# TensorE pieces planned in longer runs of one tile size, the mask in 64-column tiles, and a second layer that trails by 5 steps instead of 6

## The chip, the cores and the metric

One core of a Trainium2 chip. The metric is device time in microseconds (us) of one execution.

## The reference

Two identical layers over 2048 tokens of width 512, each a segmented attention with 32 heads of 128 and a dense relu block. The attention goes over 64 segments of 32 tokens one after the other: 8 memory rows, which are the output of the segment before, stand ahead of the 32 tokens, so each segment waits for the one before it.

```python
for s in range(n_seg):                        # 64 segments
    h = concatenate([mem, xs])                # 8 + 32 rows
    q, k, v = h @ Wq, h @ Wk, h @ Wv          # 512 -> 32 heads x 128
    p = softmax(where(mask, q @ k.T * scale, -1e9))
    o = (p @ v) @ Wo                          # 32 x 128 -> 512
    mem = o[:8]; outs.append(o[8:])
# layer: x = x + attention(layernorm(x)); x = x + relu(layernorm(x) @ w1) @ w2      (twice)
```

## The kernel before

All operations are put into a plan in Python. A greedy list scheduler then fixes the order of each engine's instructions. One **step** handles segment k of layer 0 and segment k - DELTA of layer 1 together, so 64 + DELTA steps. Query/key products are on the critical recurrence; x-values (for the next step), memory values, x output and the dense layers fill TensorE in between.

```python
DELTA = 6
LAT = (0.26, 0.16, 0.16, 0.20, 1.70)      # signal latency charged behind PE, ACT, DVE, POOL, SP
LOOK = 0.05
...
# Plan.order(): rank = longest planned path to the end
            o.rank = o.cost + LAT[o.eng] + max((s.rank for s in o.succs), default=0.0)
...
            o = max((c for c in cand[e] if c.start <= lo + LOOK), key=lambda c: (c.rank, -c.seq))
            end = o.start + o.cost
            seen = end + LAT[e]
            for s in o.succs:
                s.ready = max(s.ready, seen)
...
# PSUM: eight banks; x-values, x output, dense layers and normalization share the two of "fill"
    b_qk, b_misc, b_st, b_fill = banks("qk", 2), banks("misc", 3), banks("st", 1), banks("fill", 2)
...
# x-values: each of the four contraction slices is a piece of its own (two 64-column tiles)
        for p in range(4):
            vx = b_fill.buf()
            for c4 in range(NC4):
                def mm(vx=vx, p=p, c4=c4): ...        # 2 matmuls, 512 columns
                plan.op(PE, 0.216, mm, r=[...], w=[vx, ("vst", p)] if c4 == 0 else [vx])
...
# x output: sixteen pieces that add up in one bank (four 32-column tiles each)
        wx = b_fill.buf()
        for t in range(H // 2):
            def mm(t=t): ...                          # 4 matmuls, 512 columns
            plan.op(PE, 0.216, mm, r=[("OT", t // 4), ("OT", 4 + t // 4), ("W", "o", 3)], w=[wx])
...
# mask: one whole-array matmul (identity x mask) ahead of scores in 64-column tiles
            nc.tensor.matmul(sp[:, a_lo * 4 * L:a_hi * 4 * L], lhsT=ident[:], rhs=maskb[...], start=True, stop=False)
```

## Time and profile before

| | before |
|---|---|
| time, median of 3 runs | 2491.64 us (2477.98 to 2494.26) |
| profiled execution | 2478.0 us, granted TensorE clock 0.979 |
| TensorE / VectorE / ScalarE / GpSimd busy | 93% / 49% / 30% / 14% |

A busy TensorE is not a TensorE at its peak, because the ends of matmuls are modelled. The starts are measured, and the prediction works with them: it splits the span into start, matmul stream, tile changes and waits.

### The profile page before, as it was taken

The page shows a single profiled execution, that of the slowest core. Times are in us where ns is not written, and L with a number is a line of the kernel's source. Part 1 is how long each engine was busy: PE and PEld are TensorE (multiplying, and loading weights), DVE is VectorE, ACT ScalarE, POOL GpSimd, SP SyncE. Part 2 cuts the span into 40 slices and gives each one's busy share as a digit, 9 for nine tenths or more (in the row PEclk, how much of TensorE's full clock was granted, in tenths as well). Part 3 has the DMA queues.
Part 4 walks back from the last instruction along what each step waited for, and adds up shares of the span by engine and source line. Part 5 has one row for each costly group of instructions (what it writes and reads, how often), then busy time and mean ns, then how long its engine had stood idle before and what let it go on. Part 6 is the DMA issues. An engine that isn't in the chain of part 4 may idle for free. (4 is left out here: it accounts for less than half of the span.)

```text
span 2478.0 us, 91607 instructions
## 1 busy us (share of the span) xinstructions
PE 2300.9 (93%) x40876; PEld 1338.7 (54%) x40876; DVE 1202.9 (49%) x2947; ACT 748.5 (30%) x1818; POOL 343.9 (14%) x910
## 2 busy tenths in 40 slices
PE   0899999999999999999999999999999999999998
PEld 0455555655555554555556554655556555555554
DVE  0334455545445545554545555554555455454443
ACT  0223332332333332333333332333323332323222
POOL 2101111111111111111111111111111111111110
PEclk9899999998999999999999999999999999999999
DMA  9000111101011101110111011101111011001000
GB/s 321 16 13 13 23 24 24 24 17 28 16 24 25 23 18 23 24 28 19 22 24 28 18 23 23 24 17 28 24 24 24 17 28 24 20 18 24 15 13 17
DMA packets 39259, 71.63 MB, mean 29 GB/s; under 512 B 13168, under 2 KB 20336, under 8 KB 38864
## 3 DMA queue, kind: packets, MB, share of 16 engines
q1 hardware_dynamic: 33296, 52.34, 9.6%
q8 instruction: 320, 5.24, 0.9%
q10 hardware_dynamic: 3824, 6.78, 0.8%
q0 software_dynamic: 1744, 6.65, 0.7%
q14 instruction: 75, 0.61, 0.1%
HBM read 21.70 MB, written 2.10 MB: 10 GB/s over the span
## 5 line engine op out<-in xcount | busy, mean ns | idle before, releaser
L535 PEld LDWEIGHTS <-Wk_sb 128*128 128x128 bf16 x8960 | 350.5, 99 | 100.8 <-issue 97.7
L535 PEld LDWEIGHTS <-Wq_sb 128*128 128x128 bf16 x8960 | 352.1, 99 | 90.5 <-issue 86.6
L697 PE MATMUL fill_184<-Wo_sb,OT 128*32 128x512 bf16 x2560 | 252.5, 389 | 2.6 <-DVE xg_74 L707 1.7
L659 PE MATMUL st_182<-Wo_sb,OT 128*32 128x512 bf16 x2208 | 225.0, 406 | 3.1 <-ACT OT L442 2.2
L442 ACT CAST QT<-qk_177 128x320 bf16<-128x320 f32 (+1 forms) x279 | 112.5, 403 | 380.1 <-PE qk_177 L535 375.4
L442 ACT CAST QT<-qk_178 128x320 bf16<-128x320 f32 (+1 forms) x281 | 113.5, 404 | 354.3 <-PE qk_178 L535 353.9
L444 DVE CAST KT<-qk_177 128x320 bf16<-128x320 f32 (+1 forms) x218 | 100.3, 460 | 240.9 <-PE qk_177 L535 226.9
L444 DVE CAST KT<-qk_178 128x320 bf16<-128x320 f32 (+1 forms) x202 | 92.7, 459 | 190.3 <-PE qk_178 L535 174.2
L697 PEld LDWEIGHTS <-OT 128*32 128x32 bf16 x4480 | 112.1, 94 | 134.7 <-issue 84.9
L605 POOL TENSOR_TENSOR P_145<-es_162,sm_166 128x160 bf16<-128x160 f32 (+1 forms) x140 | 58.1, 435 | 861.3 <-ACT QT L442 397.8
L697 PE MATMUL fill_183<-Wo_sb,OT 128*32 128x512 bf16 x1920 | 170.2, 385 | 0.0
L469 PE MATMUL fill_183<-Wv_sb,XS_139 128*64 128x512 bf16 x664 | 143.5, 428 | 1.9 <-ACT hT_176 L360 1.9
L535 PE MATMUL qk_177<-HT_136,Wk_sb 128*128 128x80 bf16 (+1 forms) x2256 | 124.7, 199 | 5.0 <-POOL HT_136 L460 4.9
L535 PE MATMUL qk_178<-HT_136,Wk_sb 128*128 128x80 bf16 (+1 forms) x2224 | 122.3, 199 | 4.1 <-POOL HT_136 L460 3.9
L469 PE MATMUL fill_183<-Wv_sb,XS_138 128*64 128x512 bf16 x632 | 125.3, 399 | 0.7
L535 PE MATMUL qk_178<-HT_136,Wq_sb 128*128 128x80 bf16 (+1 forms) x2256 | 125.1, 200 | 0.3 <-DVE KT L444 0.3
L535 PE MATMUL qk_177<-HT_137,Wk_sb 128*128 128x80 bf16 (+1 forms) x2240 | 123.0, 199 | 0.0
L535 PE MATMUL qk_177<-HT_136,Wq_sb 128*128 128x80 bf16 (+1 forms) x2224 | 122.8, 199 | 0.1
L535 PE MATMUL qk_178<-HT_137,Wk_sb 128*128 128x80 bf16 (+1 forms) x2240 | 122.9, 199 | 0.0
L535 PE MATMUL qk_177<-HT_137,Wq_sb 128*128 128x80 bf16 (+1 forms) x2240 | 122.9, 199 | 0.0
L535 PE MATMUL qk_178<-HT_137,Wq_sb 128*128 128x80 bf16 (+1 forms) x2240 | 122.8, 199 | 0.0
L469 PEld LDWEIGHTS <-XS_139 128*64 128x64 bf16 x1120 | 62.9, 112 | 105.4 <-issue 94.5
(205 smaller groups left out, 3829.2 us busy)
## 6 DMA issues: line engine op xcount, KB each, us to landing
Vs_142<-vst SPq DMA_DIRECT2D x128, 128.0 KB
Vs_143<-vst SPq DMA_DIRECT2D x128, 128.0 KB
Vs_142<-vms SPq DMA_DIRECT2D x256, 16.0 KB
Vs_143<-vms SPq DMA_DIRECT2D x256, 16.0 KB
Wk_sb<-in_A_Wk_dram ACTq DMA_DIRECT2D x2, 1024.0 KB
Wv_sb<-in_A_Wv_dram POOLq DMA_DIRECT2D x2, 1024.0 KB, 18.6
Wq_sb<-in_A_Wq_dram SPq DMA_DIRECT2D x2, 1024.0 KB
Wo_sb<-in_A_Wo_dram SPq DMA_DIRECT2D x2, 1024.0 KB
```

The costliest lines, as they stand in the source:

```text
L442: nc.scalar.copy(out=out_, in_=in_)
L444: nc.vector.tensor_copy(out=out_, in_=in_)
L469: nc.tensor.matmul(vx[64 * b:64 * b + 64, :], lhsT=XS[:, c4, :], rhs=Wv_sb[:, c4, n * 512:(n + 1) * 512], start=(c4 == 0), stop=(c4 == NC4 ...
L535: nc.tensor.matmul(qp[:, hi * 2 * L:hi * 2 * L + n], lhsT=W_sb[:, c4, h * Dh:(h + 1) * Dh], rhs=HT[:, c4, c0:c1], start=(c4 == 0), stop=(c ...
L605: nc.gpsimd.tensor_tensor(out=P[:, a_lo:a_hi, :, b, 0:L], in0=es[:, a_lo:a_hi, b, :, :], in1=s.unsqueeze(3).to_broadcast([128, na, 2, L]), ...
L659: nc.tensor.matmul(wo[32 * q:32 * q + 32, :], lhsT=OT[:, h, SEG:SEG + 32], rhs=Wo_sb[:, h, :], start=(t == 0), stop=(t == H // 4 - 1), til ...
L697: nc.tensor.matmul(wx[32 * q:32 * q + 32, :], lhsT=OT[:, h, XO[a]:XO[a] + SEG], rhs=Wo_sb[:, h, :], start=(t == 0), stop=(t == H // 2 - 1) ...
```

## The change

The intent is fewer changes of the TensorE tile (whole array, 64 columns, 32 columns, 64 rows). It has four parts: (1) pieces that add up in one bank are planned as one; (2) the planner charges 0.11 us for a change of tile, and a piece on the present tile gets 2 us of rank as a bonus; (3) the mask comes as two 64-column matmuls; (4) layer 1 trails by 5 steps.

```diff
-DELTA = 6
+DELTA = 5
+WHOLE, COL64, COL32, ROW64 = range(4)
+TURN = 0.11
+STAY = 2.0
...
-            o = max((c for c in cand[e] if c.start <= lo + LOOK), key=lambda c: (c.rank, -c.seq))
+            o = max((c for c in cand[e] if c.start <= lo + LOOK),
+                    key=lambda c: (c.rank + (STAY if e == PE and c.tile == tile else 0.0), -c.seq))
...
             end = o.start + o.cost
+            if e == PE and o.tile != tile:
+                end, tile = end + TURN, o.tile
...  x-values (memory values, queries/keys, memory output, dense layers likewise)
-            for c4 in range(NC4):
-                def mm(vx=vx, p=p, c4=c4):
+            def mm(vx=vx, p=p):
+                for c4 in range(NC4):
...
-                plan.op(PE, 0.216, mm, r=[...], w=[vx, ("vst", p)] if c4 == 0 else [vx])
+            plan.op(PE, 0.216 * NC4, mm, r=[...], w=[vx, ("vst", p)], tile=COL64)
...  x output: 4 pieces in place of 16
-        for t in range(H // 2):
+        for tq in range(4):
...
-            plan.op(PE, 0.216, mm, r=[("OT", t // 4), ("OT", 4 + t // 4), ("W", "o", 3)], w=[wx])
+            plan.op(PE, 0.864, mm, r=[("OT", tq), ("OT", 4 + tq), ("W", "o", 3)], w=[wx], tile=COL32)
...  mask
-            nc.tensor.matmul(sp[:, ...], lhsT=ident[:], rhs=..., start=True, stop=False)
+            for g2 in range(2):
+                nc.tensor.matmul(sp[64 * g2:64 * g2 + 64, ...], lhsT=ident[:, 64 * g2:64 * g2 + 64],
+                                 rhs=..., start=True, stop=False, tile_position=(0, 64 * g2))
```

More of the change, by code (lines that the diff above doesn't have):

```diff
@@ L73 @@
 class Op:
-    __slots__ = ("eng", "cost", "fn", "preds", "succs", "bufs", "new", "rank", "ready", "start", "wait", "seq")
+    __slots__ = ("eng", "cost", "fn", "preds", "succs", "bufs", "new", "rank", "ready", "start", "wait", "seq", "tile")
 class Plan:
@@ L83, in available, with op @@
         self.given[key] = t
-    def op(self, eng, cost, fn, r=(), w=()):
+    def op(self, eng, cost, fn, r=(), w=(), tile=WHOLE):
         o = Op()
-        o.eng, o.cost, o.fn, o.succs, o.seq = eng, cost, fn, [], len(self.ops)
+        o.eng, o.cost, o.fn, o.succs, o.seq, o.tile = eng, cost, fn, [], len(self.ops), tile
         o.ready, preds, o.bufs, o.new = 0.0, {}, [], []
@@ L124, in order @@
                 cand[o.eng].append(o)
-        done = []
+        done, tile = [], WHOLE
         while len(done) < len(self.ops):
@@ L346, in dense_layer, with mm @@
             hp = b_fill.buf()
-            for fi, fc in enumerate(fcs):
-                fs = 128 if fc < NFC - 1 else F_LAST
-                def mm(hp=hp, fi=fi, fc=fc, fs=fs):
+            def mm(hp=hp, fcs=fcs):
+                for fi, fc in enumerate(fcs):
+                    fs = 128 if fc < NFC - 1 else F_LAST
                     for c4 in range(NC4):
@@ L354, in mm @@
                                          rhs=xnT[:, c4, :], start=(c4 == 0), stop=(c4 == NC4 - 1))
-                plan.op(PE, 0.23, mm, r=[xnT, "w1"], w=[hp, hT] if fb == 0 and fi == 0 else [hp])
+            plan.op(PE, 0.23 * len(fcs), mm, r=[xnT, "w1", *([(hT, "own")] if fb else [])],
+                    w=[hp] if fb else [hp, hT, (hT, "own")])
             nfull = sum(1 for fc in fcs if fc < NFC - 1)
@@ L372, in dense_layer, with mm @@
             fcs = list(range(4 * fb, min(NFC, 4 * fb + 4)))
-            for two in range(0, len(fcs), 2):
-                def mm(part=fcs[two:two + 2]):
-                    for fc in part:
-                        fs = 128 if fc < NFC - 1 else F_LAST
-                        nc.tensor.matmul(yp[:, :], lhsT=hT[0:fs, fc, :], rhs=w2_sb[0:fs, fc, :],
-                                         start=(fc == 0), stop=(fc == NFC - 1))
-                plan.op(PE, 0.216 * len(fcs[two:two + 2]), mm, r=[hT, (hT, fb), "w2"], w=[yp])
+            def mm(fcs=fcs):
+                for fc in fcs:
+                    fs = 128 if fc < NFC - 1 else F_LAST
+                    nc.tensor.matmul(yp[:, :], lhsT=hT[0:fs, fc, :], rhs=w2_sb[0:fs, fc, :],
+                                     start=(fc == 0), stop=(fc == NFC - 1))
+            plan.op(PE, 0.216 * len(fcs), mm, r=[hT, (hT, fb), "w2"], w=[yp])
         def add():
@@ L471, in mm @@
                                          start=(c4 == 0), stop=(c4 == NC4 - 1), tile_position=(0, 64 * b))
-                plan.op(PE, 0.216, mm, r=[("XS", i, 0), ("XS", i, 1), ("W", "v", p)],
-                        w=[vx, ("vst", p)] if c4 == 0 else [vx])
+            plan.op(PE, 0.216 * NC4, mm, r=[("XS", i, 0), ("XS", i, 1), ("W", "v", p)], w=[vx, ("vst", p)], tile=COL64)
             eng = ACT if p != 3 else DVE
@@ L498, in mem_values, with mm @@
             vm = b_st.buf()
-            for c4 in range(NC4):
-                def mm(vm=vm, pp=pp, c4=c4):
+            def mm(vm=vm, pp=pp):
+                for c4 in range(NC4):
                     for q in range(4):
@@ L505, in mm @@
                                          start=(c4 == 0), stop=(c4 == NC4 - 1), tile_position=(0, 32 * q))
-                plan.op(PE, 0.216, mm, r=[("HTm", i), ("HTx", i, 1), *[("W", "v", pc) for pc in range(4)]], w=[vm])
+            plan.op(PE, 0.216 * NC4, mm, r=[("HTm", i), ("HTx", i, 1), *[("W", "v", pc) for pc in range(4)]], w=[vm],
+                    tile=COL32)
             eng = ACT if pp == 0 else DVE
@@ L529, in queries_keys, with mm @@
             qp = b_qk.buf()
-            for h2 in range(2):
-                def mm(qp=qp, h2=h2, W_sb=W_sb):
-                    for hi in (2 * h2, 2 * h2 + 1):
-                        h = 4 * hg + hi
-                        for c4 in range(NC4):
-                            nc.tensor.matmul(qp[:, hi * 2 * L:hi * 2 * L + n], lhsT=W_sb[:, c4, h * Dh:(h + 1) * Dh],
-                                             rhs=HT[:, c4, c0:c1], start=(c4 == 0), stop=(c4 == NC4 - 1))
-                plan.op(PE, 8 * max(0.030, 0.0029 + n / 2400), mm,
-                        r=[("HTm", i), *[("HTx", i, a) for a in range(a_lo, a_hi)], ("W", nm, hg // 2)], w=[qp])
+            def mm(qp=qp, W_sb=W_sb):
+                for hi in range(4):
+                    h = 4 * hg + hi
+                    for c4 in range(NC4):
+                        nc.tensor.matmul(qp[:, hi * 2 * L:hi * 2 * L + n], lhsT=W_sb[:, c4, h * Dh:(h + 1) * Dh],
+                                         rhs=HT[:, c4, c0:c1], start=(c4 == 0), stop=(c4 == NC4 - 1))
+            plan.op(PE, 16 * max(0.030, 0.0029 + n / 2400), mm,
+                    r=[("HTm", i), *[("HTx", i, a) for a in range(a_lo, a_hi)], ("W", nm, hg // 2)], w=[qp])
             eng = DVE if nm == "k" and hg % 4 != 1 else ACT
@@ L558, in mm @@
         def mm():
-            nc.tensor.matmul(sp[:, a_lo * 4 * L:a_hi * 4 * L], lhsT=ident[:],
-                             rhs=maskb[:, a_lo:a_hi, :].unsqueeze(2).to_broadcast([128, na, 4, L]),
-                             start=True, stop=False)
+            for g2 in range(2):
+                nc.tensor.matmul(sp[64 * g2:64 * g2 + 64, a_lo * 4 * L:a_hi * 4 * L],
+                                 lhsT=ident[:, 64 * g2:64 * g2 + 64],
+                                 rhs=maskb[:, a_lo:a_hi, :].unsqueeze(2).to_broadcast([128, na, 4, L]),
+                                 start=True, stop=False, tile_position=(0, 64 * g2))
             v = spv()
@@ L595, in scores @@
         qk = [(c + "T", hg) for c in "qk" for hg in (2 * p, 2 * p + 1)]
-        plan.op(PE, 0.07 * na + 8 * na * 0.0215, mm, r=qk, w=[sp])
+        plan.op(PE, 0.07 * na + 8 * na * 0.0215, mm, r=qk, w=[sp], tile=COL64)
         plan.op(DVE, t_dve(n), top, r=[sp], w=[mx])
@@ L639, in attend @@
                 r=[("PT", p), *[("Vx", a, b) for a in range(a_lo, a_hi) for b in range(2)],
-                   *[("Vm", a, 2 * (p // 2) + b) for a in range(a_lo, a_hi) for b in range(2)]], w=pv)
+                   *[("Vm", a, 2 * (p // 2) + b) for a in range(a_lo, a_hi) for b in range(2)]], w=pv, tile=ROW64)
         for b in range(2):
@@ L654, in next_memory, with mm @@
         wo, mt = b_st.buf(), b_misc.buf()
-        for t in range(H // 4):
-            def mm(t=t):
-                for q in range(4):
-                    h = 4 * t + q
-                    nc.tensor.matmul(wo[32 * q:32 * q + 32, :], lhsT=OT[:, h, SEG:SEG + 32], rhs=Wo_sb[:, h, :],
-                                     start=(t == 0), stop=(t == H // 4 - 1), tile_position=(0, 32 * q))
-            plan.op(PE, 0.216, mm, r=[("OT", t), ("W", "o", t // 2)], w=[wo])
+        for p in range(4):
+            def mm(p=p):
+                for t in (2 * p, 2 * p + 1):
+                    for q in range(4):
+                        h = 4 * t + q
+                        nc.tensor.matmul(wo[32 * q:32 * q + 32, :], lhsT=OT[:, h, SEG:SEG + 32], rhs=Wo_sb[:, h, :],
+                                         start=(t == 0), stop=(t == H // 4 - 1), tile_position=(0, 32 * q))
+            plan.op(PE, 0.432, mm, r=[("OT", 2 * p), ("OT", 2 * p + 1), ("W", "o", p)], w=[wo], tile=COL32)
         for half, eng in ((0, ACT), (1, DVE)):
@@ L692, in project_x, with mm @@
         wx = b_fill.buf()
-        for t in range(H // 2):
-            def mm(t=t):
-                for q in range(4):
-                    h, a = 16 * (q // 2) + t, q % 2
-                    nc.tensor.matmul(wx[32 * q:32 * q + 32, :], lhsT=OT[:, h, XO[a]:XO[a] + SEG], rhs=Wo_sb[:, h, :],
-                                     start=(t == 0), stop=(t == H // 2 - 1), tile_position=(0, 32 * q))
-            plan.op(PE, 0.216, mm, r=[("OT", t // 4), ("OT", 4 + t // 4), ("W", "o", 3)], w=[wx])
+        for tq in range(4):
+            def mm(tq=tq):
+                for t in range(4 * tq, 4 * tq + 4):
+                    for q in range(4):
+                        h, a = 16 * (q // 2) + t, q % 2
+                        nc.tensor.matmul(wx[32 * q:32 * q + 32, :], lhsT=OT[:, h, XO[a]:XO[a] + SEG],
+                                         rhs=Wo_sb[:, h, :], start=(t == 0), stop=(t == H // 2 - 1),
+                                         tile_position=(0, 32 * q))
+            plan.op(PE, 0.864, mm, r=[("OT", tq), ("OT", 4 + tq), ("W", "o", 3)], w=[wx], tile=COL32)
         for a in act:
```

## The prediction

> **What bounds the kernel now.** I read the first section of the page (busy time by engine) first, then the waits of TensorE, then TensorE's timeline over two steps, and last the distances between the starts of all 40,876 matmuls.
>
> The page's first section:
>
> ```profile
> PE 2300.9 (93%) x40876; PEld 1338.7 (54%) x40876; DVE 1202.9 (49%) x2947; ACT 748.5 (30%) x1818; POOL 343.9 (14%) x910
> ```
>
> TensorE is taken all the time and no other engine passes half. The waits of TensorE, longest first:
>
> ```profile
> PE fill_183 L326 <- DVE bf_76 L321: 60.1, 1, 60.1
> PE misc_181 L614 <- POOL P_148 L605: 17.4, 6, 2.9
> PE fill_184 L326 <- DVE bf_76 L321: 14.9, 10, 3.9
> ```
>
> The first is the start of the program (the loads), once. The second is the tail of some steps: the transposes of the last quarter of the heads wait for its softmax, and there is nothing left to fill. Everything below is smaller. So the bound is what TensorE does, and the question is how much of "busy" is work. That is read from the starts in the timeline. A stretch in which the tile changes at every group, then one in which it doesn't (columns: start, length, line, tiles, shape, count):
>
> ```profile
> 1206.91 0.45 PE L535 MATMUL qk_178<-HT_137,Wk_sb 128*128 128x80 bf16 x8
> 1207.30 0.40 PE L503 MATMUL st_182<-Wv_sb,HT_137 128*32 128x512 bf16 x4
> 1207.63 0.41 PE L469 MATMUL fill_183<-Wv_sb,XS_139 128*64 128x512 bf16 x2
> 1207.96 0.40 PE L503 MATMUL st_182<-Wv_sb,HT_137 128*32 128x512 bf16 x4
> 1208.29 0.41 PE L469 MATMUL fill_183<-Wv_sb,XS_139 128*64 128x512 bf16 x2
> ...
> 1210.94 0.30 PE L559 MATMUL misc_181<-maskb,ident 128*128 128x320 bf16 x1
> 1211.17 0.38 PE L569 MATMUL misc_181<-KT,QT 128*40 128x40 bf16 x16
> ...
> 1223.45 0.39 PE L697 MATMUL fill_183<-Wo_sb,OT 128*32 128x512 bf16 x4
> 1223.66 0.39 PE L659 MATMUL st_182<-Wo_sb,OT 128*32 128x512 bf16 x4
> 1223.88 0.39 PE L697 MATMUL fill_183<-Wo_sb,OT 128*32 128x512 bf16 x4
> 1224.10 0.39 PE L659 MATMUL st_182<-Wo_sb,OT 128*32 128x512 bf16 x4
> ```
>
> Four matmuls of 512 columns in 32-column tiles take 0.22 us from start to start when the next group has the same tile (1223.45 to 1223.66 to 1223.88), and 0.33 us when the next has another (1207.30 to 1207.63 to 1207.96). Eight query/key matmuls take 8 x 36 = 288 ns among their own kind, and 0.39 us ahead of another tile. The mask matmul (320 columns, 136 ns at the same rate) is followed after 0.23 us by scores in 64-column tiles. Each change costs about 0.10 us, and the modelled busy time hides it.
>
> Done over the whole span, by the distance of starts of consecutive matmuls less the distance that the same matmul has among its own tile (36 ns query/key, 56 ns at 128 columns, 216 ns at 512, 136 ns mask, 22 ns score or value matmul; over 160 ns of excess counted as a wait), the 2478.0 us fall into: 64.3 before the first query, 1779 of matmul stream, 468 of tile changes (4,658 of them, 100 ns each) and 167 of waits. The median excess of the pairs of tiles lies between 84 and 120 ns, whichever way they change. Of the steady steps, eight in a row (1437.44 to 1720.15 us) give 35.3 us a step: 26.2 stream, 6.6 changes (67 of them), 2.3 waits. Of the waits in all full steps the largest known ender is that of the last softmax quarter (38 us over 58 steps).
>
> **What the Trainium skill says.** "TensorEngine Tiling (Array Packing)", section Key Properties: changing the tiling mode, and not just the tile, drains TensorE. The trace agrees: 100 ns a change, none between two different 32-column groups. "TensorE: Matmul & The Clock Gate", section Back-to-back issue gap, gives N/2.4 + 2.5 ns for an isolated stream, 36 ns at 80 columns and 216 at 512: the trace has 36 and 216. The same page, "Part 3: Packing small matmuls — row/col tiling", has tiles of one mode starting some 4 ns apart; here 3 ns, so two mask matmuls of 64 columns of the array should cost about what one of 128 does. "Perfetto Trace Analysis", section Tensor Engine Instruction (MATMUL, LD_WEIGHTS), says that matmul ends in a profile are estimated; hence I use starts.
>
> **The change part by part.**
>
> *Merging of planned pieces.* The matmuls stay the same in number and size; what the planner may not split any more grows. Pieces per full step before: 32 query/key, 16 x-values, 8 memory values, 4 masks, 4 scores, 4 attention, 8 memory output, 16 x output, 4 transposes of P, 1 selection, 5.5 + 3 dense, 1 transpose of x: 106, with 67 changes, 0.63 a piece. After: 16 + 4 + 2 + 4 (mask and scores are one tile now) + 4 + 4 + 4 + 4 + 1 + 1.5 + 1.5 + 1 = 47 pieces. At the same 0.63 that is 30 changes.
>
> *The bonus for staying (2 us of rank).* It lets pieces of near rank follow each other: the two memory values, x output behind memory output, scores beside x-values. It can't join everything. Query/key pieces go in pairs, since there are two banks: a piece of 16 x 36 = 0.58 us, then 0.4 to 0.46 us of eviction plus two signals, so after each pair one piece of something else goes in. Eight pairs make up to 16 changes, and the tail (transposes, four attentions in row tiles, memory output) 10 to 14 more. I take 28 a step: 39 fewer, 3.9 us a step. For the whole, 69 steps x 28 x 0.10 = 193 us in place of 468: 275 less. All of it lies on TensorE's own stream, which sets the time.
>
> *Mask in 64-column tiles.* Worth only what it removes of changes. Of 280 masks, 184 follow a whole-array matmul: the change then comes ahead of the mask instead of behind it, gain nothing. 63 follow 64-column work (2 changes less), 33 another tile (1 less): 159 x 0.1 = 16 us in the old order. It is inside the 28.
>
> *Layer 1 trails by 5.* 70 steps become 69: two single-layer steps go, one full step comes. The ten single-layer steps 1 to 5 and 64 to 68 last 27.4 us on average, a full one 35.3: 2 x 27.4 - 35.3 = 19 us in the old kernel. In the new one both shrink by about 4, so 2 x 23.4 - 31.4 = 15 us; of this the stream is 2 x 20.8 - 26.2 = 15 and the changes are already counted by 69. The price: the end of a group of layer 0 (x output, add, dense layer, two normalizations) must reach layer 1 within one step and not two. Serially I count x output 3.5 us, dense matmuls 2.5 + 2.4, and about 11 for adds, two normalizations (near 4 us each in the last steps of the trace) and the relu: 19 us. It fits into 31 us, but takes slack.
>
> *Waits.* They are 167 us now, 18 of it in the first and the last step. The old plan did not know of the changes, so its TensorE ran 6.6 us a step later than planned and the other engines had that as slack. The new plan knows of them and they are fewer: the softmax tail of a step stays as long (max, subtract, exp, sum, multiply on three engines), while what fills it is done sooner, and a shorter trail adds a burst every fourth step. I allow 3.0 us a step instead of 2.3: 69 x 3.0 + 18 = 225, which is 58 more.
>
> Sum in terms of the profiled run: 64 start + (1779 - 15) stream + 193 changes + 225 waits = 2246, against 2478, a ratio of 0.906. From the median of 2491.64 this is 2258; by the fastest 2246. I put 2250.
>
> **Rivals.**
>
> 1. *The chain of the recurrence becomes the bound.* Memory to queries, scores, softmax, attention, memory output and back is serial; the filling work only hides it. Query/key 9.3 us, scores and masks 1.6, and a tail near 9 us make 20, below 31 a step, so it should not bind as a whole; but the 2.5 to 3 us waits for the last softmax quarter in the steps at 1465 and 1537 us show it biting already. If those 3 us came in every step and the burst added as much every fourth, waits were 5 us a step: 2385.
> 2. *The gain is larger.* Were the bonus to gather runs so that 20 changes a step remain and waits stayed at 2.3: 64 + 1764 + 138 + 177 = 2143. For it: the fillers in steady steps are mostly available early (x-values a step ahead). Against: rank falls by a whole step's chain between filler and query, much more than 2 us, so the planner goes back to queries as soon as a bank is free.
> 3. *The 0.1 us is not of the tile change but of the weight load ahead of it.* Weight loads are 94 to 112 ns long by the page. If each first load of a piece were exposed it would still go with the number of runs; if it belonged to each group of four matmuls instead, nothing would be won. Against: the groups at 1223 us change weights four at a time without it.
> 4. *VectorE or ScalarE takes over.* At a step of 31 us VectorE would be at 0.52 x 35.3 / 31 = 59%. No; but larger pieces finish in a burst, so evictions queue, which is in the waits.
> 5. *Nothing gained:* the trail of 5 starves layer 1 by 10 us every fourth step (2.5 a step, 170 us) on top of rival 1. Only then does the time stay within 2%.
>
> **Range and chances.** Changes left between 20 and 36 a step mean 55 us either way; waits between 2.3 and 5 mean -50 to +138. The range is 2150 to 2350. For within 2% the time must be over 2442, so waits must eat 200 us more than I allow: chance 0.04; slower 0.01.
>
> **What would show it.** The start-to-start distances should give about 28 changes a step (1,700 to 2,100 in all) at still 0.10 us, the stream unchanged near 1764, masks started 3 ns apart in pairs with no 0.23 us behind them, query/key in runs of 16 or 32. TensorE's modelled busy time should fall with the changes. The waits for the last softmax quarter and for the normalization ahead of layer 1 should grow; if they grow beyond 5 us a step in all, or if the changes stay over 40 a step, the prediction is wrong.

## The result, and the profile after

The changed kernel takes 2096.43 us in the median of 4 runs (2091.89 to 2097.05), against 2491.15 us before. Ratios, here and below, are the mean time of one kernel's runs over that of the other's of the same rounds, so not quite the ratio of the medians: 0.8412 (0.8377 to 0.8447). It was predicted as 2250, within 2150 to 2350.

The first section of the page after the change, and TensorE's longest waits after it (columns: who waited for whom, us in total, times, longest):

```profile
PE 1959.4 (94%) x40728; PEld 1311.9 (63%) x40728; DVE 1184.2 (57%) x2913; ACT 769.5 (37%) x1795; POOL 343.8 (16%) x902
```

```profile
PE fill_183 L333 <- DVE bf_76 L328: 64.9, 3, 60.7
PE qk_178 L545 <- DVE HT_136 L694: 6.6, 3, 2.2
PE misc_180 L626 <- POOL P_147 L617: 5.8, 10, 0.7
PE qk_177 L545 <- DVE HT_136 L694: 5.1, 3, 2.2
PE fill_184 L333 <- DVE bf_76 L328: 3.4, 2, 3.1
...
PE misc_180 L626 <- POOL P_148 L617: 1.5, 3, 1.0
```

TensorE's busy share went up while the time fell by 16%: its busy time had hidden the changes. The 60 us of the start stay. The waits for the last softmax quarter, 38 us in total in the three rows of 17.4, 11.9 and 8.6 us before, are gone from the top. By what ended them, the waits for all softmax quarters went from 43 to 18 us, those for the transfers of the x-values (`Vs<-vst`) from 11 us to none listed, and those for the normalization (`bf_76`, without the start) from 15 to 8 us. The prediction had named the first and the last of these as the ones that would grow. The timeline of TensorE after (start, length, line, tiles, shape, count):

```profile
1239.85 0.74 PE L545 MATMUL qk_177<-HT_136,Wq_sb 128*128 128x80 bf16 x16
1240.52 1.05 PE L512 MATMUL st_182<-Wv_sb,HT_136 128*32 128x512 bf16 x16
1241.49 0.75 PE L545 MATMUL qk_178<-HT_136,Wq_sb 128*128 128x80 bf16 x16
1242.08 0.74 PE L545 MATMUL qk_177<-HT_136,Wk_sb 128*128 128x80 bf16 x16
...
1244.97 0.33 PE L570 MATMUL misc_180<-maskb,ident 128*64 128x320 bf16 x2
1245.13 0.36 PE L581 MATMUL misc_180<-KT,QT 128*40 128x40 bf16 x16
```

Sixteen memory-value matmuls now stand in one run, 0.97 us from 1240.52 to 1241.49: four times 0.216 and one change. Before, each four of them paid one. Query/key pieces come in pairs, and the scores follow their mask after 0.16 us (0.23 before), because the change now lies ahead of the mask.

The split of the span, measured as the prediction did, shows where it was off:

| us | before | predicted | after | after less predicted |
|---|---|---|---|---|
| start to the first query | 64.3 | 64 | 64.8 | +1 |
| matmul stream | 1779 | 1764 | 1754 | -10 |
| tile changes | 468 (4,658 x 0.100) | 193 (28 x 69 x 0.10) | 178 (1,914 x 0.093) | -15 |
| waits | 167 | 225 | 93 | -132 |
| sum | 2478 | 2246 | 2090 | -156 |

How much falls under stream and how much under waits depends on the thresholds, by 9 to 50 us from kernel to kernel.

The changes came out at 27.7 a step (1,914 / 69) where 28 was said. The waits, which were to grow by 58 us, fell by 74. That term alone is 132 of the 156 us that the sum is off, so the experiments are about the waits.

### The profile page after: what moved, and what is told of

Same layout as the page of the kernel before. It is cut to its first block, busy times and chain, and to the rows that moved or that the text cites. A ratio compares the mean times of both kernels' runs of the same rounds, so it can differ in the third digit from the quotient of the medians.

```text
span 2089.7 us, 91084 instructions
## 1 busy us (share of the span) xinstructions
PE 1959.4 (94%) x40728; PEld 1311.9 (63%) x40728; DVE 1184.2 (57%) x2913; ACT 769.5 (37%) x1795; POOL 343.8 (16%) x902
## 4 chain that ended last, share of the span: by engine, by line
PE 82%; DVE 10%; SPq 2%; DMA 2%; issue 1%; POOL 1%; ACT 1%; DVEq 0%; POOLq 0%; ACTq 0%
PE qk_178 L545 15%; PE qk_177 L545 14%; PE fill_183 L711 6%; PE st_182 L512 6%; PE fill_184 L711 6%; PE st_182 L672 6%; PE fill_184 L478 5%; PE fill_183 L478 5%; PE fill_184 L359 2%; PE fill_183 L359 2%; PE fill_183 L385 2%; PE fill_184 L385 1%; DVE KT L452 1%; PE misc_179 L646 1%; PE misc_180 L626 1%
## 5 line engine op out<-in xcount | busy, mean ns | idle before, releaser
L545 PEld LDWEIGHTS <-Wk_sb 128*128 128x128 bf16 x8832 | 333.5, 100 | 83.7 <-issue 78.1
L545 PEld LDWEIGHTS <-Wq_sb 128*128 128x128 bf16 x8832 | 329.6, 100 | 72.8 <-issue 67.3
L672 PE MATMUL st_182<-Wo_sb,OT 128*32 128x512 bf16 x2176 | 175.6, 394 | 0.0
L711 PEld LDWEIGHTS <-OT 128*32 128x32 bf16 x4416 | 104.4, 97 | 98.8 <-issue 9.7
L711 PE MATMUL fill_184<-Wo_sb,OT 128*32 128x512 bf16 x2240 | 148.2, 383 | 0.5
L711 PE MATMUL fill_183<-Wo_sb,OT 128*32 128x512 bf16 x2176 | 146.0, 386 | 0.5
L545 PE MATMUL qk_178<-HT_136,Wk_sb 128*128 128x80 bf16 (+1 forms) x2224 | 100.5, 200 | 6.6 <-DVE HT_136 L694 6.6
L545 PE MATMUL qk_177<-HT_136,Wk_sb 128*128 128x80 bf16 (+1 forms) x2256 | 101.3, 199 | 5.1 <-DVE HT_136 L694 5.1
L581 PEld LDWEIGHTS <-QT 128*40 128x40 bf16 x4096 | 93.3, 98 | 18.5 <-issue 1.0
L599 ACT ACTIVATE es_163<-es_163 128x320 f32<-128x320 f32 (+1 forms) x138 | 62.1, 450 | 111.6 <-DVE es_163 L594 110.7
L545 PE MATMUL qk_178<-HT_136,Wq_sb 128*128 128x80 bf16 (+1 forms) x2256 | 101.9, 200 | 0.1
L545 PE MATMUL qk_178<-HT_137,Wk_sb 128*128 128x80 bf16 (+1 forms) x2192 | 98.6, 199 | 2.4 <-DVE KT L452 1.3
L545 PE MATMUL qk_177<-HT_136,Wq_sb 128*128 128x80 bf16 (+1 forms) x2224 | 100.5, 200 | 0.0
L545 PE MATMUL qk_177<-HT_137,Wk_sb 128*128 128x80 bf16 (+1 forms) x2160 | 97.4, 200 | 2.2 <-DVE KT L452 1.3
L545 PE MATMUL qk_177<-HT_137,Wq_sb 128*128 128x80 bf16 (+1 forms) x2192 | 98.8, 200 | 0.0
L545 PE MATMUL qk_178<-HT_137,Wq_sb 128*128 128x80 bf16 (+1 forms) x2160 | 97.7, 200 | 0.5 <-DVE KT L452 0.5
L450 ACT CAST vst<-fill_184 128x512 bf16<-128x512 f32 x106 | 61.9, 584 | 86.5 <-PE fill_184 L478 77.2
```

What stands on the lines that cost most here:

```text
L450: nc.scalar.copy(out=out_, in_=in_)
L545: nc.tensor.matmul(qp[:, hi * 2 * L:hi * 2 * L + n], lhsT=W_sb[:, c4, h * Dh:(h + 1) * Dh], rhs=HT[:, c4, c0:c1], start=(c4 == 0), stop=(c ...
L581: nc.tensor.matmul(v[64 * g2:64 * g2 + L, a, b, ii, :], lhsT=QT[:, h, a * L:(a + 1) * L], rhs=KT[:, h, a * L:(a + 1) * L], start=False, st ...
L599: nc.scalar.activation(out=flat(), in_=flat(), func=ACTF.Exp, scale=SCALE)
L672: nc.tensor.matmul(wo[32 * q:32 * q + 32, :], lhsT=OT[:, h, SEG:SEG + 32], rhs=Wo_sb[:, h, :], start=(t == 0), stop=(t == H // 4 - 1), til ...
L711: nc.tensor.matmul(wx[32 * q:32 * q + 32, :], lhsT=OT[:, h, XO[a]:XO[a] + SEG], rhs=Wo_sb[:, h, :], start=(t == 0), stop=(t == H // 2 - 1) ...
```

## The experiments

Theories on the waits at the outset. **A**: they fell since the plan now knows of the changes, so that its order fits what happens. **B**: they fell since the pieces are longer. **C**: the trail of 5 did it. A fourth, **D**, came later: a chain of products that is not interleaved with others ends sooner, and what hangs on it starts sooner.

In the profiles of these runs tiles have no buffer numbers. The number of changes in an expectation was counted in the order of the built kernel. Eighteen kernels ran, all with correct results. The values of the profiled runs:

| run | changes | us a change | waits | x-values of a step, first to last | at half clock | ratio to before |
|---|---|---|---|---|---|---|
| before | 4,658 | 0.100 | 167 | 22.4 | 105 | 1 |
| the change | 1,914 | 0.093 | 93 | 10.3 | 53 | 0.841 |
| e1_trail5_alone | 4,384 | 0.100 | 186 | 21.5 | 128 | 0.983 |
| e2_trail6 | 2,061 | 0.093 | 50 | 8.4 | 6 | 0.829 |
| e3_no_bonus | 2,113 | 0.093 | 87 | 9.3 | 63 | 0.847 |
| e4_merged_only | 2,100 | 0.093 | 98 | 8.6 | 67 | 0.844 |
| e6_small_known | 4,480 | 0.101 | 265 | 23.1 | 221 | 1.026 |
| e8_whole_mask | 2,142 | 0.093 | 100 | 10.5 | 74 | 0.851 |
| e9_before_nolat | 3,233 | 0.096 | 117 | 18.3 | 33 | 0.909 |
| e10_small_all_nolat | 2,209 | 0.095 | 191 | 16.2 | 114 | 0.896 |
| e11_values_long | 3,161 | 0.095 | 133 | 12.6 | 71 | 0.911 |
| e12_xout_dense_long | 3,425 | 0.098 | 76 | 14.5 | 23 | 0.897 |
| e13_small_nolat_trail6 | 2,424 | 0.096 | 187 | 15.7 | 110 | 0.910 |
| e14_trail6_bonus8 | 1,681 | 0.093 | 117 | 9.4 | 40 | 0.845 |
| e15_nolat_charge | 3,219 | 0.097 | 214 | 24.0 | 105 | 0.958 |
| e17_dense_long | 4,374 | 0.101 | 174 | 20.6 | 135 | 0.986 |
| e18_trail6_nolat | 1,945 | 0.093 | 126 | 9.7 | 48 | 0.862 |
| e19_merged_only_trail6 | 2,176 | 0.093 | 140 | 11.0 | 112 | 0.875 |
| e20_trail6_bonus3 | 1,930 | 0.093 | 90 | 11.8 | 53 | 0.838 |
| e21_trail6_bonus1 | 2,031 | 0.093 | 88 | 9.3 | 39 | 0.839 |

"x-values" is the mean time in us from the first to the last x-value matmul of a step (steps 8 to 59). "At half clock" is the time in us that the trace's clock records give at half speed.

### e1_trail5_alone

```diff
 (kernel before)
-DELTA = 6
+DELTA = 5
```

> Kernel before with the trail of 5 alone. Its order has 4,384 tile changes (4,658 before). Theory A (waits fell since the plan knows the changes) and theory B (since pieces are longer): the waits of TensorE stay near 165 us, time = 65 start + 1764 stream + 438 changes + 165 = 2432 us, ratio to before about 0.98. Theory C (the trail of 5 itself took the waits away): waits near 95 us, about 2360 us, ratio about 0.95.

Measured: 2450.35 us, ratio 0.9827 (0.9786 to 0.9869), waits 186 us. C falls: the waits did not go down. The trail alone is worth 1.7%, through 274 fewer changes and 17 us less stream, and its waits grew by 19.

### e2_trail6

```diff
 (the change)
-DELTA = 5
+DELTA = 6
```

> Whole change, but the trail stays 6. 2,061 tile changes at 93 ns = 192 us, stream 1769, start 65. Theories A and B: waits near 95 us, 2121 us, ratio to before about 0.853. Theory C: waits near 167 us, 2193 us, ratio about 0.88.

Measured: 2066.69 us, ratio 0.8293 (0.8263 to 0.8323), waits 50 us. C falls again, the other way round: without part 4 this kernel is faster than the whole change, 0.829 against 0.841, each against the kernel before. Its longest wait after the start is short each time:

```profile
PE misc L626 <- POOL P L617: 15.2, 23, 1.3
PE qk L545 <- DVE KT L452: 8.1, 28, 0.4
```

### e4_merged_only

```diff
 (the change)
-TURN = 0.11
-STAY = 2.0
+TURN = 0.0
+STAY = 0.0
```

> Long pieces, mask in 64-column tiles, trail 5, but the planner charges nothing for a change and gives no bonus. 2,100 changes at 94 ns = 197 us, stream 1754, start 65. Theory A: the plan is wrong about the changes as it was before, so waits stay near 165 us: 2181 us, ratio about 0.876. Theories B and C: waits near 95 us, 2111 us, ratio about 0.848.

Measured: 2103.48 us, ratio 0.8435 (0.8399 to 0.8471), waits 98 us. A isn't needed: this plan knows as little of the changes as the old one did, and waits as little as the new one. The longer pieces (with the mask and the trail) give nearly the whole gain. With a trail of 6 it is otherwise, see e19.

### e6_small_known

```diff
 (the change, with x-value, memory-value, query/key, output and dense pieces as small as before)
-STAY = 2.0
+STAY = 0.0
```

> Small pieces as before, mask in 64-column tiles, trail 5, the planner charges 0.11 us for each change, no bonus. 4,480 changes at 100 ns = 448 us, stream 1764, start 65. Theory A: the plan is right about the changes, waits fall to about 95 us: 2372 us, ratio about 0.953. Theory B: waits stay near 165 us, 2442 us, ratio about 0.98. Theory C: as A, about 2372 us (then the run of trail 5 alone shows the low waits too).

Measured: 2555.28 us, ratio 1.0256 (1.0216 to 1.0297), waits 265 us. It is slower than the kernel before. Knowing the changes does not lower the waits of small pieces, so A falls here and B stands, but 265 is more than B said: beside the trail of 5 alone (186), the charge and the new mask made the waits worse. The row that grew is the attention's wait for the transfer of the x-values (18.2 us with the trail of 5 alone):

```profile
PE misc L647 <- DMA Vs<-vst: 63.7, 119, 2.4
```

### e9_before_nolat

Why does the old plan interleave at all? It charges the 0.26 us of a signal between any two pieces that depend on each other, even two TensorE pieces that add up in one bank. The next piece of a chain is then "ready" only 0.26 us later, and the planner puts a piece of another chain, on another tile, in between. The trace shows no such delay: in the changed kernel the sixteen memory-value products that add up in bank st_182 follow each other in 0.97 us (the run from 1240.52 us above), 0.22 us for each four and one change.

```diff
 (kernel before)
-            o.rank = o.cost + LAT[o.eng] + max((s.rank for s in o.succs), default=0.0)
+            o.rank = o.cost + max((s.rank + (0.0 if s.eng == o.eng == PE else LAT[o.eng]) for s in o.succs), default=LAT[o.eng])
-                s.ready = max(s.ready, seen)
+                s.ready = max(s.ready, end if s.eng == e == PE else seen)
```

> Kernel before (small pieces, trail 6, whole mask, no charge for a change, no bonus); the planner alone is altered: it no longer charges the 0.26 us of a signal between two TensorE pieces that depend on each other. Its order has 3,233 tile changes in place of 4,658, since a chain may now go on with its own next piece. Theory D (the waits fell because a chain of products, once begun, is finished sooner, so that its evictions and transfers start sooner): the span of the x-value chains of a step falls from 22 us to under 15 and the waits to about 100 us: 64 + 1779 + 323 + 100 = 2266 us, ratio about 0.91. Rival (only the length of the pieces or the tile knowledge does it): waits stay near 167 us, 2333 us, ratio about 0.94.

Measured: 2262.84 us, ratio 0.9092 (0.9055 to 0.9129); waits 117 us, x-values 18.3 us from first to last (under 15 was said), x output 12.2 us (24.0 before). Two lines of the planner give over half of the gain with no other part of the change. The time is as D said, the span of the x-values is only half-way there.

### e10_small_all_nolat

```diff
 (the change with small pieces as before; the two lines of e9 besides)
```

> Small pieces as before, with everything else of the change (trail 5, mask in 64-column tiles, charge of 0.11 us, bonus of 2 us) and no signal charged between TensorE pieces in the plan. 2,209 tile changes. Theory D: pieces need not be long, waits near 95 us: 65 + 1754 + 205 + 95 = 2119 us, ratio about 0.851. Rival (the length itself matters): waits near 180 us, 2204 us, ratio about 0.885.

Measured: 2231.82 us, ratio 0.8961 (0.8927 to 0.8996), waits 191 us. The rival: 2,209 changes are nearly as few as in the whole change, yet the waits are twice as long. So few changes and few waits are two things.

### e3_no_bonus

```diff
 (the change)
-STAY = 2.0
+STAY = 0.0
```

> Whole change without the bonus for staying on a tile. 2,113 changes (1,914 with it). If the bonus acts only through the changes: 199 x 0.093 = 19 us more, 2115 us, ratio about 0.849. If it also shortens chains and so waits: waits go from 93 to 120 us or more, 2140 us, ratio about 0.86.

Measured: 2104.32 us, ratio 0.8466 (0.8431 to 0.85), waits 87 us. Changes cost 19 us more and waits 6 us less. The bonus is worth less than 1%. Beside e4, which differs by the charge of 0.11 us alone, it also tests the prediction's argument on long pieces: with the charge the waits are 87 us, without it 98, and the times are the same within the noise (0.847 and 0.844). So here a plan that knows the changes does not wait more.

### e8_whole_mask

```diff
 (the change)
-            for g2 in range(2):
-                nc.tensor.matmul(sp[64 * g2:64 * g2 + 64, ...], ..., tile_position=(0, 64 * g2))
+            nc.tensor.matmul(sp[:, ...], lhsT=ident[:], ..., start=True, stop=False)
```

> Whole change, but the mask is one matmul on the whole array again; the plan takes mask and scores for one tile, so the order of everything else is the same. 2,142 changes, 228 more than with it: 21 us more if a change costs 0.093 us, 2117 us, ratio about 0.85. Rival: the change ahead of or behind the mask is hidden in waits, nothing lost: 2096 us, ratio 0.841.

Measured: 2117.55 us, ratio 0.8512 (0.8485 to 0.854). 228 more changes, which the split puts at 21 us (198.5 against 177.8), and the median is 21 us higher: the two 64-column masks cost nothing more than the one they replace, and each change saved counts in full.

### e11_values_long

```diff
 (kernel before; x-values, memory values likewise)
-            for c4 in range(NC4):
-                def mm(vx=vx, p=p, c4=c4):
+            def mm(vx=vx, p=p):
+                for c4 in range(NC4):
```

> Kernel before, with nothing but the x-value and memory-value pieces made four times longer (trail 6, no charge, no bonus). Its order has 3,161 changes (4,658 before). Theory D, sharpened: what the waits hung on are the chains that feed this step's attention, so finishing the values sooner takes away the waits for their transfers and part of those of the last softmax quarter; waits fall from 167 to about 110 us: 64 + 1768 + 316 + 110 = 2258 us, ratio about 0.907. Rival (waits depend on all pieces or on the query/key pieces): they stay near 165 us, 2313 us, ratio about 0.93.

Measured: 2267.82 us, ratio 0.9109 (0.9079 to 0.914), waits 133 us. It lies between the two: the waits fell, but by 34 us and not by 57.

### e12_xout_dense_long

```diff
 (kernel before; dense pieces likewise)
-        for t in range(H // 2):
+        for tq in range(4):
             def mm(...):
+                for t in range(4 * tq, 4 * tq + 4):
```

> Kernel before, with nothing but the x-output and dense pieces made longer. 3,425 changes. Theory D, sharpened: these chains don't feed this step's attention, so waits stay near 150 us or over: 64 + 1768 + 342 + 155 = 2329 us, ratio about 0.936. Rival: any longer chain lowers the waits to about 110 us, 2284 us, ratio about 0.918.

Measured: 2234.76 us, ratio 0.8974 (0.8939 to 0.9009), waits 76 us. The sharpened D falls: chains that do not feed the step's own attention take away more of the waits than the values do. The wait for the softmax quarters (all four, 43 us before) shrinks to

```profile
PE misc L615 <- POOL P L606: 6.6, 8, 1.4
```

In the kernel before, a chain of x output held one of the two shared banks for 24.0 us of a 35 us step (one from 1473.31 to 1503.01 us); here 9.8. The x-values, which were not touched, came down from 22.4 to 14.5 us with it.

### e13_small_nolat_trail6

```diff
 (e10)
-DELTA = 5
+DELTA = 6
```

> As the run with small pieces and all else of the change without the signal between TensorE pieces, but with the trail of 6. 2,424 changes at 0.095 us = 230 us. If it was the trail of 5 that made small pieces wait 191 us: waits about 110 us, 65 + 1768 + 230 + 110 = 2173 us, ratio about 0.873. If it was the length: waits stay near 190 us, 2253 us, ratio about 0.905.

Measured: 2265.37 us, ratio 0.91 (0.9069 to 0.913), waits 187 us. It was the length (or the planner's part with it), not the trail. The kernel with the same planner and trail and with long pieces is e18: 126 us.

### e14_trail6_bonus8

```diff
 (the change)
-DELTA = 5
-STAY = 2.0
+DELTA = 6
+STAY = 8.0
```

> Whole change with trail 6 and a bonus of 8 us in place of 2. 1,681 changes (2,061 with 2 us). If changes are all it acts on: 65 + 1758 + 156 + 50 = 2029 us, ratio about 0.815. Rival: so strong a bonus puts off the recurrence, waits double to 100 us or more and the time stays at 2079 us or over, ratio 0.835.

Measured: 2103.43 us, ratio 0.8446 (0.8419 to 0.8474), waits 117 us. The rival: 380 changes fewer than with a bonus of 2 (35 us) were given back in waits twice over (67 us against e2, whose 50 us are partly luck; 27 to 29 us against e20 and e21). The recurrence is put off:

```profile
PE qk L545 <- DVE HT L694: 25.2, 29, 1.0
```

### e15_nolat_charge

```diff
 (e9, with the tiles named)
+TURN = 0.11
...
+            if e == PE and o.tile != tile:
+                end, tile = end + TURN, o.tile
```

> The run with the kernel before and no signal charged between TensorE pieces, and besides it the planner's charge of 0.11 us a change (no bonus, whole mask, trail 6). 3,219 changes, nearly as there (3,233). If a plan that knows the changes loses the other engines' slack, as the prediction argued: waits rise from 117 to about 190 us, 65 + 1766 + 309 + 190 = 2330 us, ratio about 0.936. If not: waits stay near 117, about 2258 us, ratio 0.907.

Measured: 2387.89 us, ratio 0.9582 (0.9548 to 0.9617), waits 214 us against 117 in e9. For small pieces a plan with the changes in it does wait more, as the prediction argued, by 97 us where the prediction allowed 58. About half of it is what the prediction named: the waits for the normalization (`bf`, without the start) went from 13 to 61 us. That lost slack is the reason is not shown: the order is another as well, and its x-values take 24.0 us instead of 18.3.

### e17_dense_long

The x output alone in long pieces could not be had (the planner found no order that fits the two shared banks), so the other half of e12 was run.

```diff
 (kernel before; the dense pieces of the change, nothing else)
-            for fi, fc in enumerate(fcs):
-                def mm(hp=hp, fi=fi, fc=fc, fs=fs):
+            def mm(hp=hp, fcs=fcs):
+                for fi, fc in enumerate(fcs):
```

> Kernel before, with nothing but the dense pieces made longer. 4,374 changes. If in the run of x-output and dense pieces it was the x output (which holds one of two banks for 24 us of a 35 us step) that took the waits away: waits stay near 160 us here, 64 + 1775 + 437 + 160 = 2436 us, ratio about 0.979. If it was the dense layer: waits about 80 us, 2356 us, ratio about 0.946.

Measured: 2454.05 us, ratio 0.9857 (0.9829 to 0.9886), waits 174 us, x output still 23.3 us from first to last. The dense layer alone does nothing for the waits (time: same, at the 2% limit). Those for the softmax quarters stay at 46 us (43 before):

```profile
PE misc L615 <- POOL P L606: 46.0, 34, 2.6
```

So in e12 it was the x output that made the difference, or both together; which of the two can't be told without the run that could not be had.

### e18_trail6_nolat

```diff
 (e2, with the two lines of e9)
```

> Whole change with trail 6, and no signal charged between TensorE pieces in the plan. 1,945 changes (2,061 with the signal). If only changes matter: 65 + 1758 + 180 + 50 = 2053 us, ratio about 0.825, a little under the trail of 6 alone. Rival (a denser plan gives waits back): waits 90 us, 2093 us, ratio 0.841.

Measured: 2147.8 us, ratio 0.8622 (0.8596 to 0.8649), waits 126 us. Worse than its rival said. What gained 9% in the kernel before loses 4% here, where the pieces are long already (3% against e20 and e21).

### e19_merged_only_trail6

```diff
 (e2)
-TURN = 0.11
-STAY = 2.0
+TURN = 0.0
+STAY = 0.0
```

> Long pieces, mask in 64-column tiles, trail 6, no charge for a change, no bonus. 2,176 changes. If with long pieces the plan's knowledge and the bonus act through changes alone: 65 + 1758 + 202 + 50 = 2075 us, ratio about 0.834. If they also lower the waits: waits 100 us without them, 2125 us, ratio about 0.854.

Measured: 2177.72 us, ratio 0.8746 (0.8721 to 0.8771), waits 140 us. With a trail of 6 the plan's knowledge and bonus went with 90 us less waiting; with a trail of 5 (e4 beside the change) with 5 us. This suggested that single orders scatter.

### e20_trail6_bonus3 and e21_trail6_bonus1

```diff
 (e2)
-STAY = 2.0
+STAY = 3.0        # e21: 1.0
```

> Trail 6 with a bonus of 3 us in place of 2: 1,930 changes, 131 fewer, 12 us less. If the low waits of trail 6 (50 us) belong to it: waits 40 to 70 us, 65 + 1758 + 179 + 50 = 2052 us, ratio about 0.824. If they are a chance of one order among many: waits anywhere from 50 to 140 us, up to 2142 us, ratio up to 0.86.

> Trail 6 with a bonus of 1 us: 2,031 changes, 30 fewer, 3 us less. If the low waits belong to trail 6 with long pieces: waits 40 to 70 us, about 2061 us, ratio about 0.828. If they are a chance of one order: waits up to 140 us, up to 2150 us, ratio up to 0.864.

Measured: 2091.59 us, ratio 0.8383 (0.8357 to 0.841), waits 90 us; and 2092.66 us, ratio 0.8392 (0.8364 to 0.8419), waits 88 us. A small step of the bonus either way costs 25 us, by 40 and 38 us more of waits, so the 50 us of e2 are partly the luck of one order. Luck is not all of e19, though: its plan, which knows nothing of the changes, waits 50 us longer than these two and takes 0.875 against 0.838 and 0.839. With a trail of 6, A keeps a part that a trail of 5 did not show. Whether a trail of 6 is better than one of 5 can't be said; e2 is the best kernel that ran, and it can be kept as it is, since a built order stays.

### What the waits hang on

Ten kernels have all their pieces long (the change, e2, e3, e4, e8, e14, e18, e19, e20, e21): waits 50 to 140 us, mean 99. Seven have all small (before, e1, e6, e9, e10, e13, e15): 117 to 265 us, mean 190. So the length of the pieces goes with some 90 us of waits on average, and 40 us either way is the lottery of the order. The groups differ in other settings too, but the record holds pairs that differ by the length alone: e6 and e3 (265 and 87 us), e13 and e18 (187 and 126). In two more pairs the new mask comes with it: e1 and e4 (186 and 98), the kernel before and e19 (167 and 140). All four fall, by 27 to 178 us. This is what shows that the length lowers the waits; the size depends on the order that comes out.

How it does so is less clear. The waits go with the span of the x-values of a step (correlation 0.81 over the 20 kernels), but mostly because the two groups differ in both: within the ten it is 0.42, within the seven 0.44. And e12 with 14.5 us waits less than e18 with 9.7. The span of the x output goes with the waits still less (0.41 over all): e10 and e13 have 6.1 and 9.9 us, 24.0 before, and still wait 191 and 187 us. So a bank set free early is not enough by itself.

One wait can be followed in the trace of the kernel before, the 2.90 us ahead of 1465.39 us:

```profile
1461.02 0.41 PE L469 MATMUL fill_183<-Wv_sb,XS_138 128*64 128x512 bf16 x2
1461.47 0.58 ACT L442 CAST vst<-fill_183 128x512 bf16<-128x512 f32 x1 [3.20 <-PE fill_183 L469]
1462.08 1.17 SPq L487 DMA_DIRECT2D Vs_142<-vst  x2
1463.30 1.21 SPq L487 DMA_DIRECT2D Vs_143<-vst  x2
...
1466.30 0.19 PE L634 MATMUL misc_180<-PT,Vs_143 40*128 40x40 bf16 x1 [0.29 <-DMA Vs_143<-vst]
```

The next step's x-values would have been filling work: their input XS_139 had been there since 1420 us, and bank fill_183 was free from 1463.1. But the plan lets them start only after the transfers have read the buffer vst, and these were issued late, since the last x-value of the step came only at 1461.02. The attention itself waited for the transfer until 1466.30, and the next x-values began at 1466.50. Here a chain that ended late held back both. That this is so in the other waits is not shown.

A wait can also cost more than itself. In the kernel before, TensorE waited 2.90 us for the last softmax quarter, and then the same 512-column groups that had stood 0.22 us apart stood 0.39 and more apart:

```profile
1465.39 0.40 PE L614 MATMUL misc_181<-ident,P_148 128*128 128x128 bf16 x4 [2.90 <-POOL P_148 L605]
...
1466.50 0.41 PE L469 MATMUL fill_183<-Wv_sb,XS_139 128*64 128x512 bf16 x2
1466.74 0.39 PE L469 MATMUL fill_184<-Wv_sb,XS_139 128*64 128x512 bf16 x2
1466.95 0.60 PE L469 MATMUL fill_183<-Wv_sb,XS_139 128*64 128x512 bf16 x2
1467.34 0.64 PE L469 MATMUL fill_184<-Wv_sb,XS_139 128*64 128x512 bf16 x2
```

The stretches of the same time in numbers (bounds, length, then busy time of each engine with its instructions; the third number from the right is the granted clock):

```profile
1466.50:1471.00 4.50, 4.50 (x61) 1.62 (x56) 1.94 (x7) 0.91 (x3) 0.55 (x1) 0.62 0.02 4
1471.00:1475.00 4.00, 4.00 (x65) 1.75 (x62) 1.87 (x4) 2.23 (x5) 0.00 (x0) 1.00 0.00 0
```

The clock had dropped to half (0.62 on average over the first stretch). Matmuls at half clock fall under waits and partly under stream in the split. The table's column shows it: e2, with the fewest waits, has 6 us at half clock and 1758 us of stream; e6, with the most, 221 and 1781. The clock is the core's mean:

```profile
core 0: 2064.1 us, clock 0.999
```

```profile
core 0: 2561.4 us, clock 0.957
```

(e2 first, then e6.) The prediction left this out. As an estimate, doubling the matmuls' own distances wherever the clock record stands at half splits these off: 143 us of waits and 38 of slow matmuls before, 84 and 19 after. So most of the fall is idle time proper. Which idle time brings the clock down is not settled: the 2.90 us are one example, but in the changed kernel the drops at 308.4, 666.8 and 1383.6 us come with no gap over 0.4 us in the 6.8 us before them (by the modelled busy time), and e12 has no drop between 150 us and its last 30 us, at 76 us of waits.

## Why the prediction was right or wrong

- **Where the time was hidden: right.** 0.10 us a change, whichever way it goes, held in all 20 kernels (0.093 to 0.101). Rival 3 (weight loads) is out in the form in which nothing would be won: e10, with small pieces in longer runs of one tile, has 2,209 changes at 0.095 us. That the first load behind a change is what costs, e10 can't tell, as the prediction said, but the trace of the kernel before can: over its 4,524 changes without a long gap that load starts 2 ns ahead of its matmul in the median, while within runs of 32-column tiles the load of a next group starts 214 ns ahead. By these starts the 0.1 us pass before the load, not in it.
- **Number of changes: right.** 28 a step said, 27.7 measured; the gain by it was 290 us where 275 was said. The working by pieces held: 47 x 0.63 gave 30 without the bonus, and e3 has 30.6 (2,113 / 69); 525 of the 576 query runs are pairs. The sum is nearer than its parts, and that is luck: 12.3 changes a step lie beside query runs where up to 16 were said, 15.4 elsewhere where 10 to 14 were. The bonus matters little (e3), the length does nearly all (e4).
- **Mask: right.** 228 changes and 21 us (e8), where 16 us were said for the old order.
- **Trail: right in steps, not in what it is worth.** Stream 17 us less in e1 (15 said), and waits 19 us more there. In the whole change it can't be told from the scatter of orders.
- **Waits: wrong, and it is the step that failed.** "I allow 3.0 us a step instead of 2.3: 69 x 3.0 + 18 = 225, which is 58 more." They fell to 93. The argument was that a plan which knows of the changes loses slack. For small pieces a charge did go with more waits (e15: 117 to 214), so the direction has something to it; for long pieces it did not (e4 and e3: 98 to 87). And the argument saw only one side of the long pieces, their changes, and not that they lower the waits: by length alone from 265 to 87 us (e6, e3) and from 187 to 126 (e13, e18). The likely way is that a chain in few pieces ends sooner. Before, several chains ran side by side and ended late (x-values 22.4 us from first to last, x output 24.0), and in the wait that was followed above the late x-values held back the attention and the next filling work; in the changed kernel x-values and x output take 10.3 and 11.9 us. That way is argued from one wait and a correlation, not shown by an experiment.
- **The range: wrong by that.** The rivals let waits grow, or left them at 2.3 a step; none let them fall. With the measured waits, the sum of the other predicted terms is 64 + 1764 + 193 + 93 = 2114.

What stays open: which of the chain's effects matters most (the bank, the transfer of the values, the filler left for the tail); whether the charge acts by slack or by the order that it makes, and why it helps with a trail of 6 (e19) and not with one of 5 (e4); what brings the clock down; and the trail of 5 against 6.

## What to carry to other kernels

Read TensorE by the distances of its starts, not by its busy time: matmuls of a changed tile stood 0.1 us further apart and the profile called it busy. A plan that charges a signal between products that add up in one bank on one engine interleaves chains for nothing; make each chain one piece, or drop the charge (here not both: e18). And when filling work is made coarser, ask what ends sooner, not only what is switched less often; a greedy planner's order scatters (2067 us with a bonus of 2, 2092 with 1 or 3), so try several settings before a single one is believed.

## What the Trainium skill lacked or had wrong

- "TensorEngine Tiling (Array Packing)", section Key Properties, says that a change of mode drains TensorE but gives no time: 0.093 to 0.101 us a change in 20 kernels, and the prediction's 84 to 120 ns by pairs of tiles.
- "TensorE: Matmul & The Clock Gate", section "🔬 Part 1: The HAM clock gate (the "warmup" mystery)", has a table that puts the drop to half clock after at least one idle window of about 3.4 us (further down the page allows for short idles in another kernel, without a figure). Here, by the modelled busy time, TensorE was busy for 1.30 of the 3.41 us before the drop at 1466.98 us of the kernel before, and for 2.61 of the 3.42 us before the one at 1383.59 us of the changed kernel. So no fully idle window was needed; 6 to 221 us of a span ran at half clock in kernels of the same work.
- No page says that products which add up in one bank need no allowance for a signal between them when an order is planned: without it the same kernel had 3,233 changes in place of 4,658 and took 0.909 of the time.
